# A fused mLSTM and MLP kernel: the last steps ahead of the first products with w_in, put in another order

## The chip, the cores and the metric

The kernel runs on one core of one Trainium2 chip. That core has five engines, each with its own stream of instructions: PE multiplies matrices, DVE, ACT and POOL work on vectors, and SP issues most of the DMAs. Some DMAs come from the queues of ACT and POOL. The engines wait for one another through semaphores. The metric is the time of one execution on the device in microseconds (us); less is better.

## The reference

It has two parts. The first is an mLSTM recurrence over 768 steps for 4 x 8 heads of 40 features. The second puts the heads side by side as 3072 tokens of 320 features and runs them through a two-layer MLP:

```python
for t in range(S):
    m_new = np.maximum(f_gate[:, :, t] + m, i_gate[:, :, t])
    f_stab = np.exp(f_gate[:, :, t] + m - m_new)
    i_stab = np.exp(i_gate[:, :, t] - m_new)
    C = f_stab * C + i_stab * einsum('bhd,bhe->bhde', vt, kt)
    n = f_stab * n + i_stab * kt
    y[:, :, t] = sigmoid(o_gate[:, :, t]) * (C @ qt) / np.maximum(np.abs(n . qt), 1.0)
    m = m_new

h = x @ w_in          # 3072 x 320 by 320 x 2048
out = (h * sigmoid(h)) @ w_out
```

Both weight matrices come in as 64-bit floats, so the kernel first turns each part of them into 32-bit floats.

## The kernel before

**Units and steps.** The recurrence is cut into chunks of 64 steps. A chunk of half the heads is a unit; there are 24 of them, `u0` to `u23`. For each unit PE makes scores (`scores`, line 586), DVE weighs them by the decay matrix `D` (`weigh`, 613), PE makes the values (`values`, 641) and the state (`state`, 777 and 765), DVE normalises (`norm` and `level`, 707 to 720) and multiplies by the output gate (`scale`, 739; for `u0` this is on POOL, 735), PE transposes the result into `px` (`xpose`, 856), and ACT and DVE put it into the input of the MLP (`xputs`, 865 to 872: a copy of the first two blocks of features into `x`, and the third block split into a high half, by ACT, and the rest, by DVE, in `xb`). Three units make one step of the MLP, 384 tokens; there are 8 steps.

**The MLP.** `mm1(fc)` makes 128 of the 2048 hidden features in `ph`. In step 0 each such `ph` takes two products with a part of `w_in` (`wi`, made from `wri`), the second cut in two, which we call the main products, and then two with the tail of `w_in`, features 256 to 319 (`wh`, made from `wrc`), which we call the tail products (all on line 923). `act` then takes the tanh on ACT (937) and a product on DVE (944, `g`), and `mm2` multiplies by `w_out` into `pout` (1017). `ph` has two buffers, so `ph_2` needs the buffer of `ph_0`, which is free when `g_0` is made.

**Weights.** A part is one DMA (`wload`, 283), two ACT instructions that rearrange the 64-bit words (`rise`, 291 and 292), and one on DVE that joins them (315). A tail part is also split into a high half and the rest (`halve`, 336 and 338). `order` lists the parts: c is a tail, i a part of `w_in`, o a part of `w_out`, so `c0` is the tail and `i0` the part that `ph_0` and `ph_1` need.

**What sets the order.** Nothing is scheduled: every engine runs its instructions in the order in which the code calls them, from line 1107 on. That stretch, the head, treats `u0` to `u2` one after the other with no MLP work to fill PE. It ends with `FILL`, a table of the small work that goes between the `mm1` calls of step 0. `FILL[1]` has `u3.expo_act()`: the exponential (456) of `u3`'s matrix in the single buffer `p`, which `u3.scores()` in `FILL[2]` writes next. `gates` (lines 175 to 193) are steps of a scan over the gates, `two` being those of steps 128 to 255. `warm` and `small` put products of constants on PE, whose results nobody reads. The `dummy` products (1118) do the same at the start.

Of the kernel before, what the change touches and what calls it, by code (L numbers as in the profile page):

```python
# [31 lines left out]
DA = 32  # L32
HD1 = H * D1
KS = 64 + D
NEG = -1.0e30
LAG = 2
NBIG = 11
# [8 lines left out]
def mlstm_mlp_kernel(  # L46
# [125 lines left out]
    def gates(lo, hi):  # L172

        init = NEG if lo == 0 else m_t[:, lo - 1 : lo]
        nc.vector.tensor_tensor_scan(
            m_t[:, lo:hi], f_t[:, lo:hi], i_t[:, lo:hi], init, op0=ALU.add, op1=ALU.max
        )
        yield
        l1 = max(lo, 1)
        tt = nc.vector.tensor_tensor  # L180
        tt(out=f_t[:, l1:hi], in0=f_t[:, l1:hi], in1=m_t[:, l1 - 1 : hi - 1], op=ALU.add)
        yield
        tt(out=f_t[:, l1:hi], in0=f_t[:, l1:hi], in1=m_t[:, l1:hi], op=ALU.subtract)
        nc.vector.tensor_scalar(f_t[:, l1:hi], f_t[:, l1:hi], -120.0, None, op0=ALU.max)
        if lo == 0:
            nc.vector.memset(f_t[:, 0:1], 0.0)
        yield
        nc.vector.tensor_tensor_scan(  # L188
            LF[:, lo:hi], pat[:, lo:hi], f_t[:, lo:hi], 0.0, op0=ALU.mult, op1=ALU.add
        )  # L190
        yield
        tt(out=i_t[:, lo:hi], in0=i_t[:, lo:hi], in1=m_t[:, lo:hi], op=ALU.subtract)
        tt(out=i_t[:, lo:hi], in0=i_t[:, lo:hi], in1=LF[:, lo:hi], op=ALU.subtract)
        yield
# [69 lines left out]
    class Part:  # L264
# [17 lines left out]
                to, src = self.raw, self.src  # L282
            nc.sync.dma_start(to, src)

        def rise(self):

            if not wide:
                return
            low, high = self.raw[:, :, :, 0], self.raw[:, :, :, 1]
            h32 = high.bitcast(F32)  # L290
            nc.scalar.activation(h32, h32, AF.Prelu, scale=2.0**-112, alpha=-(2.0**32))
            nc.scalar.activation(
                low, self.raw.bitcast(U8)[:, :, :, 3], AF.Copy, scale=1 / 32, bias=-31 / 64
            )
            self.risen = True

        def make(self):
            K, nb, n, nm = self.K, self.nb, self.n, self.nm
# [76 lines left out]
        )  # L375


    order = "c0 i0 i1 o0 i2 c2 o1 i3 o2 c4 i4 o3 i5 o4 c6 i6 o5 i7 o6 o7"
    parts = [part(x[0], int(x[1])) for x in order.split()]
    nload, nmade = [0], [0]  # L380

# [3 lines left out]
    def wload(n):  # L385
        for p in parts[nload[0] : nload[0] + n]:
            p.load()
        nload[0] = min(nload[0] + n, len(parts))

    def wmake(n):  # L390

        for p in parts[nmade[0] : nmade[0] + n]:
            p.make()
            wload(1)
        nmade[0] = min(nmade[0] + n, len(parts))
# [23 lines left out]
    class Unit:  # L419
# [77 lines left out]
        def load_qk(self):  # L497
            n = self.n

            t = pb.tile([128, 2, H * L], F32, tag="big", name=f"qk{n}")  # L500
            nc.sync.dma_start(t.rearrange("p w t -> p (w t)"), qk[n])
            self.q = t[:, 0, :].rearrange("p (h t) -> p h t", t=L)
            self.k = t[:, 1, :].rearrange("p (h t) -> p h t", t=L)

# [353 lines left out]
        def xput(self, st):  # L858
            run(2, self.xputs(st))

        def xputs(self, st):
            n, px = self.n, self.px
            cs = slice(n % UPS * UT, (n % UPS + 1) * UT)
            if st.j == 0:
                nc.scalar.copy(st.x0[:, 0:2, cs], px[:, 0:2, :])
                a = slice(2, 3)
            else:
                a = slice(0, 3)
            hi, lo = st.xh[:, :, cs], st.xl[:, :, cs]
            nc.scalar.copy(hi, px[:, a, :])  # L870
            yield
            self.low = nc.vector.tensor_tensor(
                out=lo, in0=px[:, a, :], in1=hi.bitcast(F32), op=ALU.subtract
            )

    def run(n, it):
        for _ in range(n):
            next(it, None)

    def pieces(two, n):  # L880
        return (slice(0, n // 2), slice(n // 2, n)) if two else (slice(0, n),)

    class Step:


        def __init__(self, j):
            self.j = j

            if j == 0:
                self.x0 = pb.tile([128, 3, NT], F32, tag="big", name=f"x{j}")  # L890
                both = pb.tile([128, 2, NT], F32R, tag="big", name=f"xb{j}")
                self.xh, self.xl = both[:, 0:1, :], both[:, 1:2, :]
            else:
                self.xh = pb.tile([128, 3, NT], F32R, tag="big", name=f"xh{j}")
                self.xl = pb.tile([128, 3, NT], F32R, tag="big", name=f"xl{j}")
            self.g = {}
            self.po = None

        def mm1(self, fc):
            j = self.j  # L900
            fs = slice(fc * 128, (fc + 1) * 128)
            ph = psH.tile([128, NT], F32, tag="h", name=f"ph{j}_{fc}")
            if j == 0 and fc == 0:
                warm(6, ph)
            if j == 0:
                w = wi[fc // 2]
                b = fc % 2 * 128
                ops = [(w[:, a, b : b + 128], self.x0[:, a, :]) for a in range(2)]
            else:
                w = wl[fc // 2]  # L910
                b = fc % 2 * 128
                ops = []
                for a in range(2):
                    ops += [
                        (wh[:, a, fs], self.xh[:, a, :]),
                        (wh[:, a, fs], self.xl[:, a, :]),
                        (w[:, a, b : b + 128], self.xh[:, a, :]),
                    ]
            z = 2 * (j > 0)
            ops += [(wh[:, 2, fs], self.xh[:, z, :]), (wh[:, 2, fs], self.xl[:, z, :])]  # L920
            for i, (w, x) in enumerate(ops):
                for c in pieces(j == 0 and fc in (0, 1, 2, 3, 12, 13, 14) and i == 1, NT):
                    nc.tensor.matmul(  # L923
                        ph[:, c],
                        w,
                        x[:, c],
                        start=(i == 0),
                        stop=(i == len(ops) - 1),
                        skip_group_check=True,
                    )  # L930

            self.ph = ph
# [158 lines left out]
    def warm(n, to=None):  # L1091
        if to is None:
            to, m = dummy, wide_mask
        else:
            w = 1
            for x in to.shape[1:]:
                w *= x
            m = maskb[:, : w // 8].unsqueeze(1).broadcast_to([128, 8, w // 8])
        for _ in range(n):
            nc.tensor.matmul(to, identb, m, start=True, stop=True)  # L1100
# [10 lines left out]
    u1.load_v()  # L1111
    u2.load_v()
    u1.load_ko()
    wload(2)
    u2.load_ko()
    wload(2)
    for _ in range(2):
        nc.tensor.matmul(
            dummy, ident, ident.unsqueeze(1).broadcast_to([128, 4, 128]), start=True, stop=True
        )  # L1120
    two = gates(2 * L, 4 * L)
    near, far, late = spread(2 * L, 4 * L, nc.gpsimd), spread(4 * L, S), late_gates()
    widen()
# [36 lines left out]
    u1.place()  # L1160
    u1.values()
    u1.gate()
    u2.gate()
    u1.keys(nc.gpsimd)
    run(1, two)
    u1.norm()
    u1.level()
    u2.place()
    u2.values()
    u1.scale()  # L1170
    u2.keys(nc.gpsimd)
    u0.room()
    u0.xpose()
    u1.state()
    u3.mask(couple("e3")[:, :4, :].rearrange("p b (c t) -> p (b c) t", t=L))
    u3.expo()
    u2.norm()
    u2.level()
    wmake(1)
    u2.scale()  # L1180
    halve(0, nc.gpsimd)
    steps[0] = st = Step(0)
    u0.xput(st)
    u3.load_qk()
    wmake(1)
    u1.xpose()
    u3.reach()
    u1.xput(st)
    u2.room(psU, "u")
    u2.xpose()  # L1190
    u2.xput(st)
    u3.load_kvo()
    wmake(1)
    FILL = {
# [65 lines left out]
    for k in range(FIRST):  # L1260
        j, fc = divmod(k, NFC)
        st, at = steps[j], places(k)
        if j == 0 and fc in KEYS:
            units[KEYS[fc]].keys()
        st.mm1(fc)
        if 0 in at:
            def blocks():
                block(at[0].n)
                if at[0] is u3:
                    u4.exp()  # L1270

            def closes():
                if at[0] is u3:
                    u4.keys()
                close(at[0].n)

            st.act(fc, first=blocks, between=closes)
            at[0].hold()
            at[0].level()
            at[0].scale()  # L1280
            at[0].carry()
        else:
            st.act(fc, splits(k))
        if 2 in at:
            units[at[2].n + 2].exp()
            units[at[2].n + 1].misc()
        if k >= LAG:
            o = k - LAG
            steps[o // NFC].mm2(o % NFC)
        if 1 in at:  # L1290
            turn(at[1].n)
            units[at[1].n + 2].add()
        if j == 0:
            FILL[fc]()
# [260 lines left out]
```

## Time and profile before

| | us |
|---|---|
| median of 3 runs | 426.99 (426.96 to 428.1) |
| the profiled execution | 426.86 |
| its span, first to last instruction | 425.1 |
| lies around the span | 1.8 |
| PE busy | 417.6 |

The span is what the profile sees; what lies around it is the difference to the time of the same execution. All times below are us from the start of the span. A row of the timeline says when a run of equal instructions began, how long it lasted, the engine, line and operation, and, in brackets, how long the engine had been idle and what ended that. fp32 products stand in the trace as two passes each, so 16 products are printed as x32, and each pass has its own loading of weights, which is kept on a separate track (PEld).

### The profile page before, as it was taken

The page shows a single profiled execution, that of the slowest core. Times are in us where ns is not written, and L with a number is a line of the kernel's source. Part 1 is how long each engine was busy: PE and PEld are TensorE (multiplying, and loading weights), DVE is VectorE, ACT ScalarE, POOL GpSimd, SP SyncE. Part 2 cuts the span into 40 slices and gives each one's busy share as a digit, 9 for nine tenths or more (in the row PEclk, how much of TensorE's full clock was granted, in tenths as well). Part 3 has the DMA queues.
Part 4 walks back from the last instruction along what each step waited for, and adds up shares of the span by engine and source line. Part 5 has one row for each costly group of instructions (what it writes and reads, how often), then busy time and mean ns, then how long its engine had stood idle before and what let it go on. Part 6 is the DMA issues. An engine that isn't in the chain of part 4 may idle for free.

```text
span 425.1 us, 16217 instructions
## 1 busy us (share of the span) xinstructions
PE 417.6 (98%) x6864; PEld 389.7 (92%) x6864; DVE 274.5 (65%) x575; ACT 223.0 (52%) x493; POOL 131.6 (31%) x140
## 2 busy tenths in 40 slices
PE   7999999999999999999999999999999999999995
PEld 4777779999999999999999999999999999999995
DVE  5879877987875667477655677466673676444442
ACT  7787777774654454445453544454454434443331
POOL 6754235424432444034431343134530210000000
PEclk9999999999999999999999999999999999999999
DMA  8999989365533755066630774246650321001001
GB/s 267 375 358 242 282 239 287 83 174 142 130 121 98 180 150 155 26 181 179 145 99 26 191 184 133 74 137 144 163 162 2 77 56 39 20 17 32 2 2 48
DMA packets 63401, 57.60 MB, mean 136 GB/s; under 512 B 31808, under 2 KB 49936, under 8 KB 63328
## 3 DMA queue, kind: packets, MB, share of 16 engines
q1 hardware_dynamic: 63056, 56.20, 47.8%
q8 instruction: 54, 0.88, 0.9%
q10 hardware_dynamic: 208, 0.26, 0.2%
q14 instruction: 19, 0.16, 0.1%
q0 software_dynamic: 64, 0.10, 0.1%
HBM read 49.09 MB, written 7.36 MB: 133 GB/s over the span
## 4 chain that ended last, share of the span: by engine, by line
PE 77%; issue 18%; DVE 2%; ACT 1%; DMA 1%; POOL 0%; POOLq 0%; DVEq 0%; ACTq 0%
PE spot L1322 28%; PE pout L1346 26%; PE ph L923 6%; PE pout L1017 6%; PE p L586 3%; PE p L679 2%; PE p L657 2%; PE spot L765 2%; DMA home<-in_ig_dram 1%; DVE D L613 0%; PE p L856 0%; PE px L856 0%; PE po L641 0%; POOL qt L570 0%; DVE home L188 0%
## 5 line engine op out<-in xcount | busy, mean ns | idle before, releaser
L1322 PE MATMUL spot<-xh,wh 64*128 64x384 f32 x660 | 148.7, 339 | 0.0
L1346 PE MATMUL pout<-woh,gh 64*128 64x320 f32 x648 | 128.0, 311 | 0.0
L1346 PE MATMUL pout<-woh,gl 64*128 64x320 f32 x648 | 126.5, 305 | 0.0
L1346 PE MATMUL pout<-wol,gh 64*128 64x320 f32 x648 | 126.1, 304 | 0.0
L961 ACT ACTIVATE th<-spot 128x384 f32<-128x384 f32 x110 | 54.1, 492 | 132.7 <-PE spot L1322 132.5
L1322 PE MATMUL spot<-xl,wh 64*128 64x384 f32 x550 | 122.8, 336 | 0.0
L981 DVE TENSOR_TENSOR gl<-th,gh 128x384 fp32r<-128x384 f32 x113 | 75.3, 666 | 54.9 <-ACT gh L977 44.3
L968 DVE SCALAR_TENSOR_TENSOR th<-th,spot 128x384 f32<-128x384 f32 x110 | 60.6, 551 | 64.1 <-ACT th L961 64.0
L1322 PEld LDWEIGHTS spot<-xh,wh 64*128 64x128 f32 x660 | 98.8, 184 | 2.2 <-ACTq L1302 0.3
L1322 PE MATMUL spot<-xh,wl 64*128 64x384 f32 x440 | 97.7, 333 | 0.0
L1346 PEld LDWEIGHTS pout<-woh,gh 64*128 64x128 f32 x648 | 88.8, 184 | 1.3
L1346 PEld LDWEIGHTS pout<-woh,gl 64*128 64x128 f32 x648 | 88.8, 184 | 0.0
L1346 PEld LDWEIGHTS pout<-wol,gh 64*128 64x128 f32 x648 | 88.6, 184 | 0.0
L977 ACT CAST gh<-th 128x384 fp32r<-128x384 f32 x113 | 58.0, 513 | 39.0 <-DVE th L968 32.8
L1322 PEld LDWEIGHTS spot<-xl,wh 64*128 64x128 f32 x550 | 76.5, 184 | 0.0
L1322 PEld LDWEIGHTS spot<-xh,wl 64*128 64x128 f32 x440 | 64.6, 184 | 0.0
L570 POOL TENSOR_TENSOR qt<-qk,lq 104x512 f32<-104x512 f32 x22 | 29.1, 1321 | 63.1 <-ACT lq L566 62.5
L810 POOL TENSOR_TENSOR Cm<-Cm,lq 104x328 f32<-104x328 f32 x19 | 18.4, 966 | 91.0 <-PE p L679 90.0
L545 POOL TENSOR_TENSOR am<-mask,aT 128x512 f32<-128x512 f32 x20 | 20.9, 1044 | 43.2 <-DVE kw L605 19.4
L553 POOL TENSOR_TENSOR D<-D,am 128x512 f32<-128x512 f32 x20 | 27.7, 1384 | 8.9 <-DMA D<-LFd 5.9
L1017 PE MATMUL pout<-wo,g 128*128 128x320 f32 (+1 forms) x120 | 27.0, 368 | 0.0
L923 PE MATMUL ph<-x,wi 128*128 128x384 f32 (+1 forms) x78 | 23.6, 432 | 0.0
(170 smaller groups left out, 544.9 us busy)
## 6 DMA issues: line engine op xcount, KB each, us to landing
qk<-in_qk_dram SPq DMA_DIRECT2D x24, 512.0 KB, 5.2
ko<-in_ko_dram SPq DMA_DIRECT2D x24, 320.0 KB, 5.1
wro<-in_w_out_dram SPq DMA_DIRECT2D x8, 640.0 KB, 6.3
wri<-in_w_in_dram SPq DMA_DIRECT2D x8, 512.0 KB, 7.4
D<-LFl SPq DMA_DIRECT2D x32, 128.0 KB, 3.5
lq<-LFl SPq DMA_DIRECT2D x32, 128.0 KB, 4.5
vb<-in_vp_dram SPq DMA_DIRECT2D x48, 82.0 KB, 4.7
out_dram<-ob SPq DMA_DIRECT2D x45, 80.0 KB, 2.2
```

The source lines that it names most:

```text
L545: return nc.gpsimd.tensor_tensor(out=self.am, in0=mask.unsqueeze(1).broadcast_to([128, H, L]), in1=aT[:, self.c, self.p, :].unsqueeze(2).b ...
L553: nc.gpsimd.tensor_tensor(out=self.Dm, in0=self.Dm, in1=self.am, op=ALU.add)
L570: nc.gpsimd.tensor_tensor(out=self.qt, in0=self.q[:KS], in1=self.lq[:KS], op=ALU.mult)
L810: nc.gpsimd.tensor_tensor(out=v, in0=heads(Cb[r, a]) if n == NP else v, in1=self.lq[r, :, L - 1].unsqueeze(2).broadcast_to([r.stop - r.sta ...
L923: nc.tensor.matmul(ph[:, c], w, x[:, c], start=(i == 0), stop=(i == len(ops) - 1), skip_group_check=True,)
L961: self.tanh = nc.scalar.activation(th, ph, AF.Tanh, scale=0.5)
L968: nc.vector.scalar_tensor_tensor(out=th, in0=th, scalar=1.0, in1=ph, op0=ALU.add, op1=ALU.mult)
L977: nc.scalar.copy(gh, th)
L981: nc.vector.tensor_tensor(out=gl, in0=th, in1=gh.bitcast(F32), op=ALU.subtract)
L1017: nc.tensor.matmul(self.po[t][:, c], g[:, ts], w[:, c], start=(fc == 0 and i == 0), stop=(last and i == len(ops) - 1), skip_group_check=(j ...
L1322: m = nc.tensor.matmul(spot[g][:, :NT], w, x, start=(h == 0 and i == 0), stop=(h == 1 and i == n - 1), skip_group_check=True,)
L1346: m = nc.tensor.matmul(st.po[t], g[half(h), t * UT : (t + 1) * UT], w[half(h)], start=(f == 0 and i == 0 and (p, h) in ((0, 0), (0, 1), (1 ...
```

## The change

- `order` begins with `i0` and then `c0`, and SP loads `i0` ahead of `u2`'s keys and gates (`ko`), and `c0` after them.
- `rise` and `halve` can be done in two phases, and `mm1` in two ends: main products and tail products.
- In the head, ACT rearranges `i0` ahead of the gate of `u2`, and `c0` in two pieces among the copies of `xputs`. DVE scales `u1` and `u2` directly after normalising them; what it did in between (a scan step of `two`, joining `c0`) comes later. `halve` of `c0` has its high half on POOL and the rest on DVE; before, both were on POOL.
- PE transposes `u2` ahead of `u3.reach()`, makes one `warm` product where there were six, and runs the main products of `ph_0` and `ph_1`, the tail of `ph_0`, and (after `u2.state()`) the tail of `ph_1`.
- At the opening the second `dummy` product has 256 columns where it had 512, and 16 products of 16 x 16 follow it.
- q and k are loaded in 112 rows; rows 112 to 127 hold zeros and are not read.

```diff
-    order = "c0 i0 i1 o0 i2 c2 o1 i3 o2 c4 i4 o3 i5 o4 c6 i6 o5 i7 o6 o7"
+    order = "i0 c0 i1 o0 i2 c2 o1 i3 o2 c4 i4 o3 i5 o4 c6 i6 o5 i7 o6 o7"
...
-            nc.sync.dma_start(t.rearrange("p w t -> p (w t)"), qk[n])
+            nc.sync.dma_start(t[:QR].rearrange("p w t -> p (w t)"), qk[n, :QR])
...
+        def lift(self, st):
+            cs = slice(self.n % UPS * UT, (self.n % UPS + 1) * UT)
+            nc.scalar.copy(st.x0[:, 0:2, cs], self.px[:, 0:2, :])
+            self.lifted = True
...
-            if j == 0 and fc == 0:
-                warm(6, ph)
+            if j == 0 and fc == 0 and 0 in ends:
+                warm(1, ph)
...
+            main = len(ops) - 2
             for i, (w, x) in enumerate(ops):
+                if (i >= main) not in ends:
+                    continue
...
-    wload(2)
+    wload(1)
     u2.load_ko()
-    wload(2)
-    for _ in range(2):
+    wload(3)
+    for w in (4, 2):
         nc.tensor.matmul(
-            dummy, ident, ident.unsqueeze(1).broadcast_to([128, 4, 128]), start=True, stop=True
+            dummy[:, : w * 128],
+            ident,
+            ident.unsqueeze(1).broadcast_to([128, w, 128]),
+            start=True,
+            stop=True,
         )
+    for _ in range(16):
+        nc.tensor.matmul(dummy[:16, :16], ident[:, :16], ident[:, :16], start=True, stop=True)
...
     u1.gate()
+    u1.keys(nc.gpsimd)
+    parts[0].rise()
     u2.gate()
-    u1.keys(nc.gpsimd)
-    run(1, two)
     u1.norm()
     u1.level()
+    u1.scale()
     u2.place()
     u2.values()
-    u1.scale()
     u2.keys(nc.gpsimd)
+    u2.norm()
+    u2.level()
     u0.room()
     u0.xpose()
     u1.state()
     u3.mask(couple("e3")[:, :4, :].rearrange("p b (c t) -> p (b c) t", t=L))
     u3.expo()
-    u2.norm()
-    u2.level()
-    wmake(1)
+    u1.xpose()
     u2.scale()
-    halve(0, nc.gpsimd)
-    steps[0] = st = Step(0)
-    u0.xput(st)
-    u3.load_qk()
-    wmake(1)
-    u1.xpose()
-    u3.reach()
-    u1.xput(st)
     u2.room(psU, "u")
     u2.xpose()
-    u2.xput(st)
+    u3.reach()
+    steps[0] = st = Step(0)
+    x0, x1, x2 = (u.xputs(st) for u in (u0, u1, u2))
+    run(1, x0)
+    parts[1].rise((0,))
+    run(1, x1)
+    wmake(1)
+    u3.load_qk()
+    run(1, x0)
+    u2.lift(st)
+    parts[1].rise((1,))
+    run(1, x2)
+    run(1, x1)
+    wmake(1)
+    run(1, x2)
+    halve(0, nc.gpsimd, (0,))
+    halve(0, nc.vector, (1,))
+    run(1, two)
...
-        st.mm1(fc)
+        if k == 0:
+            st.mm1(0, (0,))
+            st.mm1(1, (0,))
+            st.mm1(0, (1,))
+        else:
+            st.mm1(fc, (1,) if k == 1 else (0, 1))
```

**On DVE, from the end of `u2`'s normalising to the first weights**, in the kernel before (`po_405` holds the values of `u2`, `x_464` its scaled result, `wtc` the joined tail, `wi_481` the joined `i0`, `px_428` to `px_509` the transposed `u0` to `u2`):

```order
L720 TENSOR_TENSOR po_405<-po_405,den_454 128x8x40
L315 SCALAR_TENSOR_TENSOR wtc_460<-wrc_174 128x256
L739 SCALAR_TENSOR_TENSOR x_464<-ko_178,po_405 128x256
L739 SCALAR_TENSOR_TENSOR x_464<-ko_178,po_405 128x64 x2
L872 TENSOR_TENSOR xb_473<-px_428,xb_473 128x128
L315 SCALAR_TENSOR_TENSOR wi_481<-wri_176 128x512
L872 TENSOR_TENSOR xb_473<-px_485,xb_473 128x128
L872 TENSOR_TENSOR xb_473<-px_509,xb_473 128x128
L315 SCALAR_TENSOR_TENSOR wi_522<-wri_180 128x512
```

and now:

```order
L723 TENSOR_TENSOR po_426<-po_426,den_446 128x8x40
L742 SCALAR_TENSOR_TENSOR x_479<-ko_176,po_426 128x256
L742 SCALAR_TENSOR_TENSOR x_479<-ko_176,po_426 128x64 x2
L318 SCALAR_TENSOR_TENSOR wi_511<-wri_174 128x512
L882 TENSOR_TENSOR xb_505<-px_450,xb_505 128x128
L882 TENSOR_TENSOR xb_505<-px_475,xb_505 128x128
L318 SCALAR_TENSOR_TENSOR wtc_522<-wrc_178 128x256
L882 TENSOR_TENSOR xb_505<-px_483,xb_505 128x128
L341 TENSOR_TENSOR wh<-wtc_522,wh 64x2x128 x2
L189 SCALAR_TENSOR_TENSOR home<-home 32x128
L318 SCALAR_TENSOR_TENSOR wi_538<-wri_180 128x512
```

The joining of the tail went from ahead of `u2`'s scaling to behind the second `xb`; the joining of `i0` went ahead of the first `xb`; the rest of the tail (L341) and the scan step (L189) now stand ahead of the next part of weights.

**On PE, at the first products of the MLP**, in the kernel before (six `warm` products of L1100 stand ahead of these rows; after them come the state of `u2` and the same three rows for `ph_1`):

```order
L1100 MATMUL ph_0_526<-maskb,identb 128x384
L923 MATMUL ph_0_526<-x_472,wi_481 128x384
L923 MATMUL ph_0_526<-x_472,wi_481 128x192 x2
L923 MATMUL ph_0_526<-xb_473,wh 128x384 x2
L765 MATMUL pu_u<-vb_145,kw_426 40x41 x2
```

and now:

```order
L1115 MATMUL ph_0_542<-maskb,identb 128x384
L938 MATMUL ph_0_542<-x_504,wi_511 128x384
L938 MATMUL ph_0_542<-x_504,wi_511 128x192 x2
L938 MATMUL ph_1_547<-x_504,wi_511 128x384
L938 MATMUL ph_1_547<-x_504,wi_511 128x192 x2
L938 MATMUL ph_0_542<-xb_505,wh 128x384 x2
L768 MATMUL pu_u<-vb_145,kw_443 40x41 x2
```

The main products of `ph_1` went ahead of the tail products of `ph_0`.

## Rows read from the trace of the kernel before

**Rows 1.** The page's head: span, and busy time of each engine with its share.

```profile
span 425.1 us, 16217 instructions
PE 417.6 (98%) x6864; PEld 389.7 (92%) x6864; DVE 274.5 (65%) x575; ACT 223.0 (52%) x493; POOL 131.6 (31%) x140
```

**Rows 2.** Chain of waits from 28 to 80 us, its shares by line.

```profile
by line: PE ph L923 44.1%; PE pout L1017 42.1%; PE p L586 4.9%; PE p L679 3.2%; PE p L657 2.6%; PE p L856 1.9%; PE pu_u L765 1.1%; PE pu_h L765 0.7%
```

**Rows 3.** Timeline of PE, 24 to 28 us: pout of fc 0, scores of u3.

```profile
25.89 1.78 PE L1017 MATMUL pout<-wo,g 128*128 128x320 f32 x6
27.77 0.69 PE L586 MATMUL p<-qk 40*64 40x64 f32 x32
```

**Rows 4.** Timeline of ACT, 22 to 28 us, from the first tanh to u3's exponential.

```profile
22.16 0.49 ACT L937 ACTIVATE th<-ph 128x384 f32<-128x384 f32 x1 [1.03 <-PE ph L923]
...
27.11 0.60 ACT L456 ACTIVATE D<-e 128x512 f32<-128x512 f32 x1
```

**Rows 5.** Timeline of PE around the first products of the MLP.

```profile
13.39 0.73 PE L641 MATMUL po<-vb,D 128*64 128x82 f32 x16
14.68 0.79 PE L641 MATMUL po<-vb,D 128*64 128x82 f32 x16 [0.55 <-DVE po L707]
...
18.89 0.55 PE L856 MATMUL px<-ident,x 128*128 128x128 f32 x3
...
20.25 1.53 PE L923 MATMUL ph<-x,wi 128*128 128x384 f32 x6
21.47 0.65 PE L923 MATMUL ph<-xb,wh 128*128 128x384 f32 x2
```

**Rows 6.** Timeline of DVE, from the weighing of u2 to the weights i0.

```profile
13.11 0.68 DVE L613 TENSOR_TENSOR D<-p,D 128x512 f32<-128x512 f32 x1
13.70 0.79 DVE L188 TENSOR_TENSOR_SCAN home<-home 32x128 f32<-32x128 f32 x1
14.42 0.14 DVE L707 TENSOR_SCALAR po<-po 128x8 uint32<-128x8 uint32 x1
...
15.63 0.68 DVE L739 SCALAR_TENSOR_TENSOR x<-ko,po 128x256 f32<-128x256 f32 x3
16.23 0.17 DVE L707 TENSOR_SCALAR po<-po 128x8 uint32<-128x8 uint32 x1
...
17.39 0.42 DVE L315 SCALAR_TENSOR_TENSOR wtc<-wrc 128x256 uint32<-128x256 uint32 x1
17.73 0.68 DVE L739 SCALAR_TENSOR_TENSOR x<-ko,po 128x256 f32<-128x256 f32 x3
...
19.11 0.98 DVE L315 SCALAR_TENSOR_TENSOR wi<-wri 128x512 uint32<-128x512 uint32 x1 [0.49 <-ACT wri L292]
...
21.17 0.69 DVE L315 SCALAR_TENSOR_TENSOR wi<-wri 128x512 uint32<-128x512 uint32 x1 [0.68 <-ACT wri L292]
```

**Rows 7.** Timeline of ACT: copy of the transposed blocks of u2.

```profile
19.47 0.37 ACT L865 COPY x<-px 128x256 f32<-128x256 f32 x1
```

**Rows 8.** Timeline of PE at the opening.

```profile
1.36 3.71 PE L1118 MATMUL dummy<-ident 128*128 128x512 f32 x4 [1.36 <-POOL ident masks.py:199]
4.92 0.81 PE L433 MATMUL e<-maskb,identb 128*128 128x512 bf16 x3
5.66 0.69 PE L586 MATMUL p<-qk 40*64 40x64 f32 x32
6.29 1.11 PE L1104 MATMUL dummy<-maskb,identb 128*128 128x64 bf16 x32
8.21 0.39 PE L442 MATMUL e<-terms,home 96*128 96x64 bf16 x8 [0.82 <-DVE terms L170]
```

**Rows 9.** Window from 2 to 5 us: length; busy time and instructions of each engine, clock, DMA share, GB/s.

```profile
2.00:5.00 3.00, 3.00 (x5) 0.91 (x4) 1.05 (x4) 2.90 (x9) 2.65 (x7) 1.00 0.97 308
```

**Rows 10.** DMA queue of kind instruction on the page, whole span: transfers, MB, share.

```profile
q8 instruction: 54, 0.88, 0.9%
```

**Rows 11.** The same queue from 11.9 to 12.3 us.

```profile
q8 instruction: 1, 0.02, 17.0%
```

More of the change, by code (lines that the diff above doesn't have):

```diff
@@ L34 @@
 KS = 64 + D
+QR = 112
 NEG = -1.0e30
@@ L283, in load, with rise @@
             nc.sync.dma_start(to, src)
-        def rise(self):
+        def rise(self, phases=(0, 1)):
             if not wide:
@@ L290, in rise @@
             h32 = high.bitcast(F32)
[L291 to L295, printed above, removed]
+            if 0 in phases:
+                nc.scalar.activation(h32, h32, AF.Prelu, scale=2.0**-112, alpha=-(2.0**32))
+            if 1 in phases:
+                nc.scalar.activation(
+                    low, self.raw.bitcast(U8)[:, :, :, 3], AF.Copy, scale=1 / 32, bias=-31 / 64
+                )
+                self.risen = True
         def make(self):
@@ L864, in xputs @@
             if st.j == 0:
-                nc.scalar.copy(st.x0[:, 0:2, cs], px[:, 0:2, :])
+                if not hasattr(self, "lifted"):
+                    self.lift(st)
                 a = slice(2, 3)
@@ L895, in __init__, with mm1 @@
                 self.xl = pb.tile([128, 3, NT], F32R, tag="big", name=f"xl{j}")
-            self.g = {}
+            self.g, self.made = {}, {}
             self.po = None
-        def mm1(self, fc):
+        def mm1(self, fc, ends=(0, 1)):
             j = self.j
             fs = slice(fc * 128, (fc + 1) * 128)
-            ph = psH.tile([128, NT], F32, tag="h", name=f"ph{j}_{fc}")
-            if j == 0 and fc == 0:
-                warm(6, ph)
+            if 0 in ends:
+                self.made[fc] = psH.tile([128, NT], F32, tag="h", name=f"ph{j}_{fc}")
+            ph = self.made[fc]
+            if j == 0 and fc == 0 and 0 in ends:
+                warm(1, ph)
             if j == 0:
```

## The prediction

> **What bounds the kernel now.** I read the head of the page first: PE is busy for 417.6 of 425.1 us [rows 1], so the end moves only with PE's work or its idle time. The chain of waits from 28 to 80 us comes next: every line in its shares is one of PE [rows 2], and no other engine takes any of it. From the scores of `u3` on the kernel is one row of PE work, and the change adds none to it. So the time is the start of `u3.scores`, 27.77 [rows 3], plus a constant: 426.86 - 27.77 = 399.1 with the 1.8 that lies around the span. The question is only what sets that 27.77.
>
> For this I read the timelines of PE and ACT side by side. `pout` on PE runs from 25.89 for 1.78, to 27.67 by the row, and the scores follow at 27.77 [rows 3]. They write the buffer `p`, which ACT's exponential reads from 27.11 to 27.71 [rows 4]. That exponential was not late for want of input: it stands at the end of a row of ACT work without a gap, from the first tanh at 22.16 on, which itself waited 1.03 us for PE's `ph` [rows 4]. From there to the end of the exponential are 27.71 - 22.16 = 5.55 us. ACT does the same work in the same order there after the change. So the 27.77 follows the first tanh, and that follows the tail products of `ph_0`, by 22.16 - 21.47 = 0.69 [rows 4, 5]. When PE starts the main products (20.25 [rows 5]) does not matter by itself.
>
> **The change part by part.**
>
> *Ahead of the main products.* The reordering on DVE takes two things out of the chain. The scan of 0.79 stood in it: the values that `norm` takes start at 13.39 and end, by 0.73, at 14.12, and `norm` started at 14.42, when DVE was through with the scan [rows 5, 6]. Without it `norm` starts near 14.20, which is 0.22 gained. The rest of the first normalising is 15.63 - 14.42 = 1.21, so scaling `u1` starts at 15.41; 16.23 - 15.63 = 0.60 later comes the second normalising, at 16.01; it takes 17.39 - 16.23 = 1.16, to 17.17. There the joining of the tail stood, 17.73 - 17.39 = 0.34 [rows 6]. It is gone too, so scaling `u2` starts at 17.17 and not 17.73: 0.56 earlier. It takes 0.68, to 17.85. PE's transpose takes 0.55 [rows 5], to about 18.45 with the handover; it now stands ahead of `u3.reach()`. ACT's copy takes 0.37 [rows 7], to 18.85. In the meantime DVE joins `i0`: 0.69 if POOL leaves it alone, as in the later row, 0.98 as it was in the first [rows 6], so 18.5 to 18.8. The main products start at 18.95, where they started at 20.25 [rows 5]: 1.3 us earlier. That counts only if the first tanh moves.
>
> *The tail products.* They now stand behind the main products of `ph_1`, which cost what those of `ph_0` do: 21.47 - 20.25 = 1.22 [rows 5]. So the tail starts at 18.95 + 2 x 1.22 = 21.39, against 21.47, and the tanh at 22.08, against 22.16. The gain of 1.3 is paid back with 1.22; what is left is -0.08. The high half and the rest of the tail, now on POOL and DVE, have until 21.39. Joining the tail comes behind `i0` and two `xb` on DVE, and I put the rest of it at 20.9, half a microsecond ahead. If this cover were gone, each microsecond of lateness would be one at the end.
>
> *Moved and covered.* The scan goes behind this, and its results are read by nothing before 22. The next part of weights on DVE then slips from 21.17 by about 0.5, also ahead of its first reader (`ph_2`). On SP, `i0` now passes `u2`'s gates, which land later behind it, and ACT's gate of `u2` must be ready by 17.17. It has most of a microsecond in hand. On ACT the pieces of the tail stand among the copies and have until 20. On POOL the keys of `u1` stand one place earlier, and a DMA issued behind the scan comes a microsecond later for a reader past 27.77. All of these I cost at nothing, up to 0.3 if the first of them fails.
>
> *Fewer warm products.* PE gets five fewer, and has no gap in their place that is longer than the 0.55 us it stood still at 14.12; the products after that gap took 0.79 for 16, against 0.73 ahead of it [rows 5]. So no price.
>
> *q and k.* Each of 24 loads shrinks by an eighth. The products read 40 of the rows, and PE waits for no load after 28 us. At the opening the first load may land up to 0.5 earlier, but the scores are not late there; DVE's terms are (0.82 idle at 8.21 [rows 8]). Nothing.
>
> *The opening.* Four `dummy` passes of 512 columns take 3.71 [rows 8]: 0.93 each. Half of two is cut: -0.93. Added are 16 products of two passes. The nearest row is the 32 `small` products of 64 columns, 1.11 in all [rows 8]; doubled for the slower pace, 2.2; with passes of 16 columns I take half of that, 1.1. So +0.17 between -0.4 and +1.3, in front of 0.82 of idle time [rows 8] that takes it up to +0.5 beyond. I cost it at nothing.
>
> The sum: -0.08 from the tanh, nothing from the rest, so 426.8, which I round to 426.9, in view of the next paragraph's small losses. The profiled execution lies 0.13 below the median of 426.99.
>
> **The rivals.**
>
> *Instructions arrive late (+0.3 to +0.7).* PE stopped for 0.55 us from 14.12 [rows 5]. The row names `norm`, but `norm` ends only 0.12 ahead of the start and what those values need, the weighed `D`, was ready at 13.79 [rows 6]. The page shows 54 transfers of instructions, 0.88 MB, so 16 KB each [rows 10], and 13,728 products and loadings on PE [rows 1]: 254 to a transfer. One of them ran at 12 us [rows 11]. I read the stop as PE at the edge of a transfer that came late under full DMA load. The 16 small products add 64 instructions, which move each edge 64 ahead: this one to the state of `u0`, and the next one to the first main products of `ph_0`, where a stop is on the path. It may be 0 to 0.7 there, and as it is the same chain the stop at 14.12 may also go. At worst 427.6, most likely 427.3. In the Trainium skill, *Runtime: NRT & Kernel Launch*, section "Instruction fetch mechanics", blocks are 16 KiB or 256 instructions, as these rows have it, and the crossing is "mostly hidden". By that page this rival costs nothing, and the stop at 14.12 speaks against it.
>
> *The start of the main products counts (425.6).* If `u3.scores` did not depend on the tanh but on PE's own row, PE's start 1.3 earlier would reach the end: 426.86 - 1.3 = 425.6. For it: PE is the bound everywhere else [rows 2], and by the row `pout` ends only 0.1 ahead of the scores [rows 3]. Against it: the gapless row of ACT [rows 4]. That a part of the 0.1 is gained is in the forecast's range.
>
> *The clock at the opening (428.7, the other side).* The `dummy` passes take 1.81 ns for a column, the main products 1.22 us for 1536 columns, 0.79 [rows 5, 8]: PE runs at 1.2 GHz up to 4.92 and at 2.4 GHz from there on, though the granted clock in this stretch reads 1.00 [rows 9]. What ran ahead of the rise was wide passes back to back. The change puts 32 tiny passes in place of a part of them. If the rise then comes after `small`, the masks (0.74), the scores (0.63) and `small` (1.11) take twice their time [rows 8]: +2.5, and with +0.2 from above and 0.82 of cover, +1.9, which all of the chain behind `terms` takes over: 428.7. It decides from the point where the rise is over 0.8 late. For it: no row shows the rise with tiny passes ahead of it. Against it: the wide ones still run for 2.8 us ahead of them.
>
> **How the numbers follow.** Forecast, no change, 426.9: 0.62, own range 426.4 to 427.2. Late instructions: 0.18. Clock: 0.09. Start of the main products: 0.07. The remaining 0.04 is something I don't see, either way. A measurement of this kernel tells about 0.3%, or 1.28 us, from no change. The first two lie within it. The third is over it; of the fourth, 425.6 is just over. So faster 0.08, same 0.81, slower 0.11. The range is 425.9 to 428.1: it leaves out the full price of the clock and the full gain of the fourth, 0.16 with parts of the unknown.
>
> **What would show it.** In the changed kernel: the main products near 18.95 and the first tanh near 22.1; the exponential of `u3` again 5.0 us behind it, with no gap on ACT; PE idle for a microsecond or so ahead of `u3.scores`, which shows that the 1.3 is lost there; the masks at 4.9 or earlier with 0.25 us a pass; DVE's terms at 8.2 unmoved. A stop of PE with nothing late ahead of it, at the state of `u0` or within the first main products, would show late instructions. I am wrong if the tail's high half or rest comes after 21.4, if the exponential ends before the tanh plus 5.5, or if the scores of `u3` start when `pout` ends.

## The result, and the profile after

| | before | after |
|---|---|---|
| median, us | 427.04 (426.60 to 429.33, 22 runs) | 430.47 (427.08 to 433.13, 22 runs) |
| ratio | | 1.0062 (95%: 1.0046 to 1.0079) |
| the profiled execution | 426.86 | 428.04 |
| its span | 425.1 | 426.3 |

The changed kernel is slower by 0.6%, outside the range of the prediction (425.9 to 428.1). The ratio agrees with that of the means; the medians alone would give 1.0080. The new number here is the scatter: 6 us between single executions, 2.7 before. So one profile doesn't tell this case; the one of the changed kernel is among its shorter executions.

The head of its page answers to [rows 1]. PE is as busy as before, plus the new products:

```profile
span 426.3 us, 16269 instructions
PE 418.7 (98%) x6891; PEld 390.0 (91%) x6891; DVE 274.6 (64%) x577; ACT 223.2 (52%) x493; POOL 129.9 (30%) x138
```

The timeline of PE in the same execution answers to [rows 3, 5] (start, how long, operation; in brackets idle time and what ended it):

```profile
13.07 0.77 PE L780 MATMUL pu<-vb,kw 128*40 128x82 f32 x16 [0.23 <-issue]
13.64 1.33 PE L644 MATMUL po<-vb,D 128*64 128x82 f32 x32
...
19.33 2.75 PE L938 MATMUL ph<-x,wi 128*128 128x384 f32 x12
21.79 0.64 PE L938 MATMUL ph<-xb,wh 128*128 128x384 f32 x2
...
28.06 0.69 PE L589 MATMUL p<-qk 40*64 40x64 f32 x32 [0.64 <-ACT D L459]
...
44.27 0.55 PE L859 MATMUL p<-ident,x 128*128 128x128 f32 x3 [0.21 <-DVE x L742]
...
296.02 0.41 PE L1381 MATMUL pout<-woh,gl 64*128 64x320 f32 x2 [0.20 <-issue]
```

And ACT, against [rows 4]:

```profile
22.47 0.49 ACT L952 ACTIVATE th<-ph 128x384 f32<-128x384 f32 x1 [1.72 <-PE ph L938]
...
27.41 0.60 ACT L459 ACTIVATE D<-e 128x512 f32<-128x512 f32 x1
```

The main products start 0.92 earlier than before, the tail products 0.32 later, the tanh 0.31 later, and the scores of `u3` 0.29 later (28.06 against 27.77). Aligned instruction by instruction, the execution loses 0.29 there, another 0.44 at 44 us and another 0.45 at 296 us: together the 1.2 of the span. The last two lie where the prediction looked for nothing.

### The profile page after: what moved, and what is told of

Same layout as the page of the kernel before. It is cut to its first block, busy times and chain, and to the rows that moved or that the text cites. A ratio compares the mean times of both kernels' runs of the same rounds, so it can differ in the third digit from the quotient of the medians.

```text
span 426.3 us, 16269 instructions
## 1 busy us (share of the span) xinstructions
PE 418.7 (98%) x6891; PEld 390.0 (91%) x6891; DVE 274.6 (64%) x577; ACT 223.2 (52%) x493; POOL 129.9 (30%) x138
## 4 chain that ended last, share of the span: by engine, by line
PE 71%; issue 18%; DMA 8%; SPq 1%; DVE 1%; POOL 1%; ACT 0%; POOLq 0%; DVEq 0%; ACTq 0%
PE spot L1357 28%; PE pout L1381 26%; PE pout L1032 4%; PE ph L938 4%; PE p L589 3%; PE p L682 2%; DMA wro<-in_w_out_dram 2%; DMA wri<-in_w_in_dram 2%; PE p L660 2%; DMA D<-LFd 2%; DMA qk<-in_qk_dram 2%; PE spot L768 2%; SPq L284 0%; PE p L859 0%; POOL qt L573 0%
```

## The experiments

Medians, with their number of runs; a verdict needs the interval. The executions of the kernel before that ran beside these experiments have medians of 427.15 to 427.38 (427.04 beside the result above).

**The changed kernel again (`again`, 12 runs).**

> The changed kernel once more, nothing edited. In its profiled execution PE's masks at 5.19 us still ran at half pace (1.46 for three passes, 0.81 before), and PE came to full pace at 6.7 us where the kernel before did at 4.9. That execution took 428.0; the median is 430.5. Clock theory: in a slower execution the rise comes later still, or PE falls back after it, and the profile of one would show stretches at half pace worth the 2 to 3 us; times from 427 to 433 again. Rival, that the reordered head sets the 430: PE's pace would be full from 7 us on in every execution, and the time would lie in idle stretches of PE after 20 us.

428.78 (427.12 to 432.74), ratio 1.0050 (1.0025 to 1.0075). The profiled execution took 427.12 and is the one in which nothing stops PE ahead of the tanh. It is the prediction's own course: forecast 18.95, 21.39 and 22.08.

```profile
18.96 2.75 PE L938 MATMUL ph<-x,wi 128*128 128x384 f32 x12
21.41 0.65 PE L938 MATMUL ph<-xb,wh 128*128 128x384 f32 x2
```

```profile
22.11 0.49 ACT L952 ACTIVATE th<-ph 128x384 f32<-128x384 f32 x1 [1.73 <-PE ph L938]
```

**The opening put back (`old_opening`, 10 runs).** In the changed kernel:

```diff
-    for w in (4, 2): (the second dummy product 256 columns wide)
-    for _ in range(16): (the small products)
+    for _ in range(2): (512 columns each)
```

> The changed kernel with the opening of the kernel before: two dummy passes of 512 columns, no small products. Clock theory: full pace from 4.9 us, and the scattered 428 to 433 becomes 427.3 to 427.6 with a spread like that of the kernel before. What stays over 427.0 is the stop at 44 us (0.44), where POOL's transfer of the scanned gates comes 1.7 late. The stop of 0.23 at the state of u0 goes, and one of some 0.5 at 14 us (ahead of the values of u2) comes back, since all instructions are 64 further up. Rival, the reordered head sets the time: the median stays at 430.

429.23, ratio 1.0050 (1.0025 to 1.0074): the loss stays. In its profile PE waited 1.23 for DVE's terms at 8.81, and the stop that was expected back at 14 us did not come.

**The new opening alone (`new_opening`, 12 runs)** is the same edit the other way, in the kernel before:

> The kernel before with the opening of the changed kernel alone: second dummy cut to 256 columns, 16 small products. Clock theory: median 429 to 431, scattered over 4 us or more, PE at half pace beyond 5 us. The stop at 14.1 moves to the state of u0. Rival, the reordered head sets the time: 427.0 as before, with the spread of before.

427.50 (426.02 to 429.89), ratio 1.0007 (0.9990 to 1.0023). The theory that the clock at the opening sets the loss falls with both: the opening alone costs nothing in the median, and without it the loss stays. What the new opening does shows in its shortest executions (426.02 against 426.59 among the 27 of before beside it). The stop of 0.55 at 14 us is gone there, and the first tanh comes at 21.46, not 22.16:

```profile
21.46 0.49 ACT L937 ACTIVATE th<-ph 128x384 f32<-128x384 f32 x1 [0.96 <-PE ph L923]
```

Against 22.11 in `again`, which has the same opening and no stop either, the reordered head costs 0.65. Against `qk128` (further down), which has the same rows as well and reaches the products with `terms` at 8.21 as against 8.19, it is 0.75 (22.21). The stop in the kernel before had hidden that.

**The scan earlier (`scan_earlier`, 6 runs).** `old_opening` with

```diff
     halve(0, nc.gpsimd, (0,))
+    run(1, two)
     halve(0, nc.vector, (1,))
-    run(1, two)
```

> As old_opening, and the scan step of two on DVE stands ahead of the rest of the tail and not behind it. DVE idles 0.3 us there, waiting for POOL, so the tail comes no later. If the stop at 44 us is POOL's late transfer (issued at 22.3 where it was at 20.6), the transfer goes out near 21, the stop of 0.44 is gone, and the time is 0.3 to 0.5 under old_opening, near 427.0. If the stop has another cause, it stays and the time is that of old_opening.

429.48, ratio 1.0055 (1.0035 to 1.0074): no gain in the median, but the stop at 44 us is gone. That the late scan had made it is not shown. In the profile of the changed kernel POOL's transfer of the scanned gates does wait 1.22 for DVE's scan (it was issued at 20.62 before),

```profile
22.29 0.80 POOL L241 DMA_DIRECT2D LFd<-home  x1 [1.22 <-DVE home L189]
```

but it lands at 28.3, and SP comes to the first transfer that reads it only at 28.6. SP stands still at the second of them, and all that is behind it in SP's queue with it (the two took 1.41 before):

```profile
28.61 2.82 SPq L495 DMA_DIRECT2D D<-LFd  x2
```

What it waits for there is a part of `w_out`, by SP's waits from 20 to 45 us:

```profile
SPq L495 <- DMA wro<-in_w_out_dram: 1.9, 1, 1.9
```

This part was issued at 21.70 and landed at 30.96; in the kernel before, at 20.69 and 29.12, and SP waited 0.5. `qk112` (further down), which has the scan where the kernel before has it, waits 2.6 at this place and has the stop as well, 0.29 long at 44.29. In the three profiles with 112 rows, the scan ahead and no such stop, PE itself was 1.0 to 2.3 later there than in the kernel before, so the same lateness of the loads would not show.

The profile of `scan_earlier` has a stop of another kind, at 15.14, 0.82 long:

```profile
15.14 0.79 PE L644 MATMUL po<-vb,D 128*64 128x82 f32 x16 [0.82 <-DVE den L715]
```

**A longer execution (`again2`, 8 runs), and the scan earlier in the changed kernel (`after_scan`, 12 runs).**

> The changed kernel a third time, for a profile of one of its slower executions. Its runs so far lie between 427.1 and 433.1; the two profiles are of 428.0 and 427.1. In both the exponential of u3 starts 0.6 after pout ends, and there are stops at edges of instruction transfers (0.2 at 13 us, 0.4 at 296 us). Theory clock: in an execution over 430 PE's pace falls to half for a stretch inside the span, or rises later than 7 us, worth 2 to 3 us. Theory edges: it is more and longer stops at edges, up to 1 us each, at full pace.

> The changed kernel with one edit: the scan step of two ahead of the rest of the tail on DVE. In scan_earlier this took the stop at 44 us away (idle PE there 0.64 to 1.38 in three profiles, none with the scan ahead). Edges of instruction transfers lie as in the changed kernel. Theory that this wait is a main part: median 0.5 to 1.3 under the changed kernel, 428 to 429.5. Theory clock or edges: less than 0.5.

`again2`: 430.11, ratio 1.0071 (1.0043 to 1.0100), profile of 429.87. `after_scan`: 429.84, ratio 1.0030 (0.9999 to 1.0061), profile of 429.56. By the medians the earlier scan gives 0.2 against the 430.08 of all 42 executions of the changed kernel; the intervals of the ratios overlap. In both profiles PE stands at the same place, the state of `u0`, first in `again2`, where the stop at 46 us follows, then in `after_scan`, where it doesn't:

```profile
14.34 0.77 PE L780 MATMUL pu<-vb,kw 128*40 128x82 f32 x16 [1.58 <-POOL ko L566]
...
46.44 0.55 PE L859 MATMUL p<-ident,x 128*128 128x128 f32 x3 [1.12 <-DVE x L742]
```

```profile
15.01 0.77 PE L780 MATMUL pu<-vb,kw 128*40 128x82 f32 x16 [2.08 <-POOL x L738]
```

The names in brackets differ, and what these products need, the keys `kw` from POOL, was ready at 10.5 and 10.7. What is common is the count of instructions. Counted in the trace's records of PE (passes, loadings of weights and waits), both stops come after 448 of them. The stops at 296.02 in the changed kernel (10,176), at 15.14 in `scan_earlier` and at 14.68 before (450 each) lie whole multiples of 256 from there, within two, and the one at 46 us doesn't (1,234). The transfer for that block ran at 11.75 for 1.2 in `again2`,

```profile
q8 instruction: 1, 0.02, 12.5%
```

(the window from 11.6 to 12.2), and PE went on 1.4 after its end, as it did in the kernel before (12.18 + 1.09 + 1.41 = 14.68), in the changed kernel (1.37) and in `after_scan` (1.39). So the length of the stop follows the start of the transfer: 10.2 in `again`, 10.5 in the changed kernel, 11.75 and 12.5 in these two, for stops of 0, 0.23, 1.58 and 2.08. These stops are most of what the two executions lose: `u3.scores` starts at 29.33 in `again2`, 1.56 behind the kernel before, of 3.0 in the span, and at 29.98 in `after_scan`, 2.21 of 2.7.

In the Trainium skill, *Runtime: NRT & Kernel Launch*, section "Instruction fetch mechanics", the crossing of such a block is "mostly hidden". Over the 54 blocks that holds; at the few here it doesn't.

**More warm products (`warm6`, 12 runs), and the edges moved (`pad40`, 12 runs).**

> The changed kernel with six warm products ahead of the first MLP products, as before, and five of the 32 small products fewer, so that from there on every instruction lies at the same place in its transfer as in the changed kernel. The main products come up to 0.6 later, and so may the first tanh. Theory clock (it falls where PE idles at 19 us): no time over 430 any more, median 428.5 to 429. Theory edges: median stays near 430, some 0.5 more for the later tanh.

431.58, ratio 1.0086 (1.0058 to 1.0114): it doesn't help, so PE's idle time at 19 us is not the cause.

> scan_earlier with ten 16 x 16 products behind its dummies, 40 instructions, in front of 1.2 us in which PE waits for DVE's terms. By the times at which PE reached the edges in scan_earlier, the shortest run of 256 instructions grows from 2.6 to 3.3 us, and block 16 (stops of 0.54 and 1.03 at 134 us in the two kernels without the shift) from 2.8 to 3.6. Theory edges: the stop at 134 us gone, that at 14 us moved or shorter, median 1 to 2 us under the 429.5 of scan_earlier. Theory that the reordered head itself costs it: the same 429.5.

429.49, ratio 1.0059 (1.0038 to 1.0080). The stop at 134 us went, as worked out, and a stop of 1.53 in the middle of the state of `u0`, where no product waits for anything, took its place (the transfer began at 13.2). Moving edges does not remove the cause. Something makes the transfers late.

**The rows of q and k.** In the windows of the profiles all kernels keep the DMA engines at a share of 1.0, but move different amounts. Columns: stretch; length; busy time and instructions of PE, PEld, DVE, ACT and POOL; clock, DMA share, GB/s. The kernel before:

```profile
2.00:10.00 8.00, 7.18 (x107) 3.83 (x105) 4.74 (x15) 6.21 (x15) 5.22 (x15) 1.00 1.02 328
...
20.00:30.00 10.00, 9.90 (x105) 7.46 (x104) 7.35 (x17) 8.80 (x21) 6.68 (x7) 1.00 1.05 364
```

The changed kernel:

```profile
2.00:10.00 8.00, 8.00 (x139) 4.68 (x137) 4.64 (x15) 6.24 (x15) 5.34 (x15) 1.00 1.03 277
...
20.00:30.00 10.00, 9.18 (x100) 6.45 (x98) 7.89 (x18) 8.11 (x20) 6.83 (x8) 1.00 1.05 322
```

As busy, and 12 to 16% fewer bytes. In the packet records, a packet of 4096 bytes (a row of q and k) takes 0.182 us on average before 10 us in the kernel before, and 0.232 in the changed one: 384 x 0.182 = 69.9 us of engine time for three loads became 336 x 0.232 = 78.0. It is these packets that are slow: from 10 to 20 us they take 0.164 to 0.169 in the six profiles with 128 rows and 0.208 to 0.234 in eight with 112, while those of 2560 bytes take 0.112 to 0.120 and 0.114 to 0.118. Four kernels undo or do this edit alone:

```diff
-            nc.sync.dma_start(t.rearrange("p w t -> p (w t)"), qk[n])
+            nc.sync.dma_start(t[:QR].rearrange("p w t -> p (w t)"), qk[n, :QR])
```

> The kernel before with one edit: q and k loaded in 112 rows. The prediction had this at nothing, by 64 KB less in each load. In the traces a packet of 4096 bytes of q and k takes 0.18 to 0.19 us in both kernels with 128 rows and 0.22 to 0.25 in all eight with 112, so three loads of 112 packets take longer than three of 128. Theory rows: the whole early DMA comes 0.5 to 1 later, with it the instruction transfer that PE needs at 14 us; median 428.5 to 430, and packets of 0.22 or more. Theory order (the reordered head alone sets the loss): 427.0 to 427.3.

> The changed kernel with q and k in 128 rows. Theory rows: packets back at 0.18 to 0.19, the instruction transfer starts by 11 us in most executions, the stop at the state of u0 goes from 1.5 to 2.1 (in the slower executions) to below 0.5, and the median from 430 to 427.5 to 428.3. What remains is the tail products behind ph_1 (0.65 in the tanh against new_opening without stops) and POOL's late transfer. Theory order: 429.5 or more.

> The changed kernel with the opening of before and 128 rows: the reordered head is all that is changed. Theory rows: 427.3 to 428.3, the stop at 44 us under 0.5. Theory order: 429 as old_opening, which differs from it only in the rows.

> qk128 with the scan step ahead of the rest of the tail. Theory rows: 0 to 0.4 under qk128, 427.2 to 428, no stop at 44 us. If it lies under the kernel before, the reordered head is worth having without the 112 rows.

| 128 rows | median (runs) | 112 rows | median (runs) |
|---|---|---|---|
| kernel before | 427.38 (35) | `qk112` | 428.45 (12) |
| `qk128` | 427.95 (12) | changed kernel, three studies | 430.08 (42) |
| `order_only` | 428.07 (12) | `old_opening` | 429.23 (10) |
| `qk128_scan` | 427.48 (12) | `after_scan` | 429.84 (12) |

Each line is one edit (the medians of a line can be of different studies, in which the kernel before lay within 0.34). The 112 rows cost 1.1 to 2.4 us in all four, or 1.0 to 2.2 by the ratios. With 128 rows no interval leaves out the kernel before, though all three medians lie above it, by 0.1 to 0.7, so a small loss by the reordered head stays possible (`qk128` 1.0011, 0.9987 to 1.0035; `qk128_scan` 1.0007, 0.9984 to 1.0030; `order_only` 1.0027, 0.9999 to 1.0056). `qk112` alone is unclear by its interval (1.0023, 0.9991 to 1.0056); the other lines and the next runs decide it. The instruction transfer that PE needs near 14 us starts at 9.3 to 10.1 in five of the six profiles with 128 rows, but at 12.18 in that of the kernel before, and at 10.2 to 13.2 in the nine with 112; `qk112`, at 12.25, does not show the delay that was expected of it. With 128 rows the same stretch of the changed kernel moves

```profile
2.00:10.00 8.00, 8.00 (x138) 4.68 (x137) 4.77 (x15) 6.20 (x15) 5.30 (x15) 1.00 1.00 312
...
20.00:30.00 10.00, 9.18 (x100) 6.46 (x98) 8.01 (x17) 8.13 (x19) 6.57 (x8) 1.00 1.05 362
```

and PE has no stop at the state of `u0`, and `u3.scores` at 27.80, where the prediction had them:

```profile
12.80 0.77 PE L780 MATMUL pu<-vb,kw 128*40 128x82 f32 x16
...
27.80 0.69 PE L589 MATMUL p<-qk 40*64 40x64 f32 x32 [0.64 <-ACT D L459]
```

How far late data reaches shows the profile of `qk112`, of 432.1. ACT waits 2.20 for a part of `w_out`, DVE's product is late, PE stands for 2.69, and then runs at 1.2 GHz for a stretch, by the granted clock of 0.51:

```profile
53.40 0.80 ACT L292 ACTIVATE wro<-wro 128x640 f32<-128x640 f32 x1 [2.20 <-DMA wro<-in_w_out_dram]
```

```profile
59.37 2.93 PE L924 MATMUL ph<-x,wi 128*128 128x384 f32 x4 [2.69 <-DVE g L945]
```

```profile
59.00:62.50 3.50, 3.13 (x6) 1.92 (x7) 3.33 (x11) 0.00 (x0) 0.03 (x1) 0.51 1.04 229
```

`qk64_48`, one of the next runs, shows it after a stop of 3.08 at 48.12:

```profile
48.10:51.60 3.50, 3.48 (x8) 2.27 (x9) 2.82 (x5) 2.73 (x6) 0.96 (x1) 0.52 0.90 190
```

A stretch like this takes the mean granted clock of an execution to 0.996. Of the 42 executions of the changed kernel 16 have a mean under 0.997, with a median of 431.2; the other 26 have 428.6. So the theory of the clock, as it was put for executions over 430, is not refuted: 15 of the 21 over 430 are among those 16, and the profile of `again2` is of 429.87. None of the 16 was profiled, so what PE had stood still for in them is not shown.

**Other numbers of rows**, in the kernel before (`qk120`, `qk104`, `qk64_48`, 4 runs each; the last as two transfers).

> The kernel before with q and k in 120 rows. If the price of the packets hangs on the rows not filling the 16 DMA engines in equal blocks of eight, a packet takes 0.20 to 0.25 here as well; if only on 112, it is back at 0.18 to 0.19. With 0.22 a load of 120 packets is worse than both others, and the time 428 or more.

> The kernel before with q and k in 104 rows, 416 KB a load. If a packet takes as long as in 112 rows (0.22 to 0.25), 104 of them take 23 to 26 us of engine time against 23.3 for 128 at 0.182: the time is between 427 and 428.5. If a load in fewer rows simply lasted shorter in proportion, packets would be at 0.18 and the time at 427 or under.

> The kernel before with q and k in 112 rows, but as two transfers of 64 and 48 rows, four and three for each DMA engine. If the price hangs on how a single transfer of 112 rows falls on the engines, packets come back to 0.18 to 0.19 and the time to 427.0 to 427.6; if on the rows as such, 0.22 and 428.5. The second transfer costs SP some 0.4 us of issue in each of three early loads either way.

431.47 (ratio 1.0107, 1.0073 to 1.0142), 431.23 (1.0085, 1.0062 to 1.0107) and 432.90 (1.0121, 1.0094 to 1.0148). Packets took 0.286, 0.267 and 0.274 us, longer than any of the expectations had it. All are clearly slower, the 104 rows too, which move a fifth less than 128.

```profile
2.00:10.00 8.00, 8.00 (x107) 4.15 (x105) 4.66 (x15) 6.23 (x15) 5.29 (x15) 1.00 0.96 238
```

That is `qk104`: 238 GB/s against 328. In the Trainium skill, *DMA: Bandwidth & Descriptors*, section "Why a DMA increments its semaphore by 16 and not by 1", a load is spread over the largest number of engines up to 16 that divides its rows. By that 104 rows use 13, 120 use 15, and 112 use all 16. No run here shows the engines one by one; but 112 rows are slow as well, and so are 64 and 48, so a smaller number of engines is not the whole of it. (`qk64_48` also issues each load twice, so of it only the packets speak to this.) Why the packets take longer stays open.

**The exponential earlier (`qk128_scan_exp`, 12 runs).**

```diff
-        1: lambda: (run(2, near), wmake(1), u3.expo_act(), u3.keep(), ...
+        1: lambda: (run(2, near), u3.expo_act(), u3.keep(), wmake(1), ...
```

> qk128_scan with the exponential of u3 ahead of the next part of weights on ACT, 1.1 us earlier. The prediction says that u3's scores wait for it (0.6 of idle PE ahead of them in seven profiles of the reordered head) and that the end follows. If so, the scores start when pout ends and the median falls by 0.4 to 0.6, to 426.9 to 427.1. If the wait is given back later (the part of weights is 0.6 late on ACT), 427.5 as qk128_scan.

427.75, ratio 1.0016 (0.9994 to 1.0038). The scores now follow `pout` without the 0.64 of idle time, which shows that it was the exponential that they waited for:

```profile
25.14 1.96 PE L1032 MATMUL pout<-wo,g 128*128 128x320 f32 x6
27.04 0.69 PE L589 MATMUL p<-qk 40*64 40x64 f32 x32
```

The profiled execution took 426.76. But the gain is gone 6 us later. DVE's joining of the part of weights began at 28.05 and took 1.51, the rest of the next tail was late behind it, and PE waited for that:

```profile
32.93 0.61 PE L938 MATMUL ph<-xb,wh 128*128 128x384 f32 x2 [0.45 <-DVE wh L341]
```

The next `pout` began at 33.38, where the kernel before has it at 33.40: the wait was given back later, as the second half of the expectation has it. No version here beats the kernel before.

## Why the prediction was wrong, step by step

- **"q and k ... Nothing."** This is the step that failed. The number of bytes was taken for the cost. The four pairs put the price at 1.1 to 2.4 us: in a head where the DMA share is 0.97 from 2 us on [rows 9], slower packets make everything late that is only just in time. The prediction even allowed for a first load up to 0.5 earlier; its last packet ended at 4.55, against 4.45 before. With 128 rows the changed kernel's median, 427.95, lies inside the range of the prediction. What carries the price to the end differs from one execution to the next, and is shown only for those profiled: the instruction transfer (2.21 of 2.7 in `after_scan`), the wait for a part of `w_out` at 44 us, the clock after a long stop (`qk112`).
- **"Instructions arrive late (+0.3 to +0.7)."** Right in mechanism and place (the edge moved to the state of `u0`, and the stop at 14.12 went with it), wrong in size. I took the delay of one execution for fixed. It is 0 to 2.1, by the start of the transfer: with 128 rows 0 in five profiles and 0.55 in that of the kernel before.
- **"A DMA issued behind the scan ... at nothing."** Not refuted. The loss at 44 us is 0.1 to 1.3 in five profiles with 112 rows and the late scan (0.44 in the changed kernel's) and nothing in `qk128` and `order_only`, where the scan is as late; `qk112` has 0.5 with the scan ahead. What SP waits for there is a part of `w_out`, which comes late behind the other loads (issued 1.0 later, after a part of `w_in` that landed 1.0 later).
- **What bounds the kernel** held: the gapless row of ACT, 5.54 us from the tanh to the end of the exponential after (28.01 - 22.47) against 5.55, and the scores behind it. `qk128_scan_exp` took the bound away and the scores moved. What did not hold is that behind the scores there is only PE's work: from their start to the end the prediction had 399.1, the changed kernel's profile has 428.04 - 28.06 = 400.0, by the stops at 44 and 296 us, and in `qk128_scan_exp` a wait for weights took the gain back.
- **The sum of the head** held where PE was not stopped: 18.96, 21.41 and 22.11 against 18.95, 21.39 and 22.08. That it fits to 0.03 is partly luck: `again` reached the products with `terms` at 8.04 and not 8.21, and DVE stood still for 0.20 ahead of scaling `u2`, which the sum did not have. `qk128`, with 8.21, has 19.07, 21.53 and 22.21. But the stop at 14.12 in the kernel before was on its path; without it, the old order has the tanh 0.65 to 0.75 earlier. "No change" compared a head without a stop to one with it.
- **The clock at the opening.** In the profile of the changed kernel the masks did take 1.46 and not 0.81, at half pace up to 6.6 us. The idle time of 0.82 took it up whole: PE reached the products with `terms` at 8.18. So the price was nothing, and `new_opening` confirms it. The clock that falls later, behind a long stop, stands in no term of the prediction.
- **"Start of the main products"** (425.6): refuted. They started 0.92 to 1.29 earlier, and PE idled 0.64 ahead of `u3.scores`.

The range missed because the one term with a price was excluded without a row: no profile of before had a load of fewer than 128 rows of this width, and the term was not bounded on the side of a loss at all.

## What to carry to other kernels

Where the DMA share is 1.0, count a smaller load by the time of its packets, not by its bytes, and try it alone before it goes in with other edits: here 128 full rows were faster than 112, 104 or 120. Where PE runs at its bound, its instructions are a transfer too. Blocks of 256 instructions last 2.5 to 16 us here, those ahead of the stops at 13 and 296 us 5.1 and 3.9, and inserted instructions move every edge behind them. And when single executions scatter by more than before, look at several profiles for what differs between them; the shortest one shows the planned course, and the longer ones show the price.

## What the runs showed that was not expected

- A packet of 4096 bytes: 0.181 to 0.188 us on average ahead of 10 us in six profiles with 128 rows, 0.219 to 0.252 in nine with 112, 0.267 to 0.286 in 104, 120, and 64 and 48 rows.
- At the stops near 14 us PE went on 1.4 us after the end of the instruction transfer that it waited for, in seven profiles (1.36 to 1.41); 1.21 in `pad40`, 1.48 in `warm6` and 1.53 in `qk112`.
- PE's full pace began anywhere from 4.4 to 7.5 us, with either opening, and PE fell back to 1.2 GHz for 3.5 us after it had stood for 2.7 us (`qk112`), 3.1 (`qk64_48`) and 2.0 (`qk104`), but not after 2.1 in `after_scan` (granted clock 1.00 from 15 to 20 us).
